# A one-token attention and feed-forward kernel: looping the query stage and the first head, loading w_down early, multiplying the last V rows directly

## The chip, the cores and the metric

The kernel runs on one core of one Trainium2 chip. The metric is device time in microseconds (us) of one execution. Engines are PE (TensorE), VectorE (DVE in the profile), ScalarE (ACT), GpSimd (POOL) and SyncE (SP), and the core has 16 DMA engines. The profile's span, from the first to the last instruction, was 1.8 to 2.1 us shorter than the time of the same run in the profiles told here.

## The reference, cut to what matters

```python
xn = _layernorm(x)                        # x: 1 x 448
q  = xn @ wq                              # 16 query heads of 256
scores = q . k_cache * 256 ** -0.5        # 8 key heads x 65536 x 256, bfloat16: 268 MB
o  = softmax(scores) . v_cache            # another 268 MB
A  = o @ wo
y  = (silu(xs @ w_gate) * (xs @ w_up)) @ w_down * sigmoid(xn @ w_r)   # one token, so xs = xn
out = x + A + xn + y
```

Almost all bytes are the two caches, each read once: 537 of the 549 MB that the DMA engines move. The arithmetic per byte is small.

## The kernel before

A key head is worked on in U = 4 units of 128 rows on each of 128 partitions. K and V pass through a ring of four 4 MB slots. SyncE issues a load when its slot has been freed (`FREE`). K is transposed on PE (`k_T`), copied out of PSUM by VectorE and ScalarE, and multiplied by the query (`k_QK`, `k_JT`). Phase A is the scores of the first head, phase B mixes a V unit of one head with a K unit of the next, phase C is V of the last head.

```python
def slot_item(kd, u, c, parts=None):      # one 4 MB load; waits until the ring slot was freed
    ...
    item(..., [("FREE", r - NSLOT)] if r >= NSLOT and k == 0 else ())

item("wq", [(w_area[:, 0:WQN], flat_src(A_wq, WQN), "wq")])
for u in range(U):                        # order of loads: wq, K of the first head ...
    for c in range(HC):
        slot_item("k", u, c)
    if u == U // 2 - 1:                   # ... with w_gate, w_up, half of w_down in the middle
        item("wg", [...], [("QT",)])
        item("wd_a", [(wd_a[:, :], wd_src(0), "wd")])
for t in range(NT):                       # then K, a pair of V slots, K
    slot_item("k", t + U, 0)
    pair_item(t)
    ...
item("wd_b", [(w_area[:, 0:WDN], wd_src(1), "we0")], [("FFN1",)])   # last loads of all:
for i in range(rep):                                                # w_down's second half, wo
    item(("wo_end", i), ...)

# The query stage: 112 matmuls, unrolled, every address fixed
for b in range(n):
    rr, c = divmod(b, 2 * half)
    ...
    ins = mm(ps_m[0:P, C_Q + lo:C_Q + lo + half + 1:half],
             lhsT=w_area[:, o:o + Dh].rearrange("p (x f) -> p x f", f=NH)[:, :, c % NH],
             rhs=xnT_sb[:, x0:x0 + 2], start=(b == 0), stop=(b == n - 1), skip_group_check=True)

def turn_A(u):                            # phase A on PE: a loop over pairs of units
    first = (u // 2) * 2 * SETS
    for c in range(HC):
        k_slots(sets_of(u, c), first)
    if u % 2:                             # the pipeline is emptied after every second unit
        n = (u + 1) * SETS
        k_JT(n - 2); k_QK(n - 1); k_JT(n - 1)

def ending():                             # (cut) after the last V rows
    dve_ob(T)                             # copy the accumulators out of PSUM
    pe_oT(T)                              # transpose, scale
    pe_ffn2(1, "wd_b", w_area)            # y, second half: 7 matmuls
    ...                                   # base row += y
    for i in range(rep):
        W_item("pe", ("wo_end", i))
        O("pe", ("FIN", i), lambda it, i=i: attn_mm(ps_fin, wo_end[:, :], [i], i == 0, i == rep - 1))
    ...                                   # RESULT = ps_fin + base row; one store from SyncE
```

## Time and profile before

| what | value |
|---|---|
| time, median of four runs | 1282.55 us (1282.35 to 1282.99) |
| DMA | 549 MB at 429 GB/s, 16 engines busy from 1.8 us to about 1272 us |
| PE / VectorE / ScalarE busy | 76% / 46% / 36% |
| first V pair issued | 101.75 us |
| last load (second part of wo) landed | 1275.7 us |
| end of the span | 1281.15 us |

The page's slices of the kernel before (40 equal slices of the span; a digit is the busy share in tenths, the last row is the DMA rate):

```profile
span 1281.2 us, 22851 instructions
DMA  9999999999999999999999999999999999999997
GB/s 406 424 436 424 450 426 427 431 431 439 436 438 417 437 430 441 432 430 428 432 446 426 436 424 436 430 444 430 428 428 433 441 436 430 425 435 431 434 437 310
```

The DMA row is full up to the last slice. The Trainium skill (DMA: Bandwidth & Descriptors, Specifications) gives a fabric ceiling of 435 GB/s; 429 over the whole span agrees with it. So time can be won only after the last bytes, and it is lost wherever the queue has nothing to do.

The timeline of PE in the kernel before, at the start (start in us, length, engine, line, operation, output and inputs, count, and in brackets the idle time before it with what ended it):

```profile
13.90 3.15 PE L367 MATMUL ps_m<-xnT_sb,w_area 128*128 128x2 bf16 x112 [1.63 <-ACT xnT_sb L355]
22.79 5.59 PE L367 MATMUL ps_t<-ident_f,ring 128*128 128x128 f32 x32 [5.74 <-DMA ring<-in_A_k_cache_dram]
...
71.06 5.35 PE L367 MATMUL ps_t<-ident_f,ring 128*128 128x128 f32 x32 [4.14 <-DMA ring<-in_A_k_cache_dram]
```

The query stage takes 3.15 us, or 28 ns per matmul. Then PE waits 5.74 us for keys, and later, before the third unit, another 4.14 us. Between those two waits PE is the slower partner: a set of 16 transposes comes every 2.53 us, a slot has four sets, so 10.1 us a slot, while a slot's 4.19 MB take 9.8 us at 429 GB/s. In phase A PE therefore never catches up by itself. The ring and the loads queued ahead hide that.

The tail of the kernel before, from the timeline (weight loads and interleaved lines left out):

```profile
1272.80 0.60 PE L367 MATMUL ps_o<-ring,p_sb 128*4 128x512 bf16 x4 [0.66 <-DMA ring<-in_A_v_cache_dram]
1273.45 0.69 DVE L555 CAST ob_sb<-ps_o 100x512 bf16<-100x512 f32 x1 [50.85 <-PE ps_o L367]
...
1274.69 2.77 PE L367 MATMUL ps_t<-w_area,hT_sb 128*1 128x448 bf16 x7 [0.22 <-DMA w_area<-in_B_w_down_dram]
...
1277.26 1.70 PE L367 MATMUL ps_s<-wo_end,oT_sb 128*1 128x448 bf16 x4
...
1278.99 0.61 DVE L742 TENSOR_TENSOR res_bf<-ps_s,rowsf 1x448 bf16<-1x448 f32 x1 [0.82 <-PE ps_s L367]
1279.63 0.32 SPq L791 DMA_DIRECT2D out_dram<-res_bf  x1
```

Eviction, w_down's matmuls, output matmuls, addition and store follow one another, 8.35 us from the release of the last V rows to the end.

### The profile page before, as it was taken

How to read it: one execution, taken by the hardware profiler on the slowest of the kernel's cores; microseconds unless marked ns; L12 is line 12 of the kernel's file. 1: busy time of each engine (PE TensorE's matmuls, PEld its weight loads, DVE VectorE, ACT ScalarE, POOL GpSimd, SP SyncE). 2: the span in 40 equal slices, each digit the busy share in tenths (PEclk: the TensorE clock that was granted, in tenths of full speed). 3: DMA queues.
4: the chain of work that ended last, by engine and by line, in shares of the span. 5: the costliest groups of instructions: out<-in, count | busy, mean ns of one | idle time of the engine just before them, and what ended most of it. 6: DMA issues, size and time to landing. Idle time of an engine off the chain costs nothing.

```text
span 1281.2 us, 22851 instructions
## 1 busy us (share of the span) xinstructions
PE 971.8 (76%) x9824; PEld 668.1 (52%) x9824; DVE 584.6 (46%) x1091; ACT 459.4 (36%) x655; POOL 4.5 (0%) x35
## 2 busy tenths in 40 slices
PE   3988777788777778677797678786778876777845
PEld 3867555455454555454664445554445644445511
DVE  4756444454444454344554344553345543445300
ACT  2645333353333443224443233432334433334300
POOL 1000000000000000000000000000000000000000
PEclk9988887898888898878888889988898888889776
DMA  9999999999999999999999999999999999999997
GB/s 406 424 436 424 450 426 427 431 431 439 436 438 417 437 430 441 432 430 428 432 446 426 436 424 436 430 444 430 428 428 433 441 436 430 425 435 431 434 437 310
DMA packets 17908, 549.22 MB, mean 429 GB/s; under 512 B 1891, under 2 KB 3942, under 8 KB 4710
## 3 DMA queue, kind: packets, MB, share of 16 engines
q1 hardware_dynamic: 17890, 549.04, 99.5%
q8 instruction: 8, 0.13, 0.0%
q14 instruction: 6, 0.05, 0.0%
q10 hardware_dynamic: 4, 0.00, 0.0%
HBM read 549.03 MB, written 0.00 MB: 429 GB/s over the span
## 4 chain that ended last, share of the span: by engine, by line
DMA 69%; PE 30%; SPq 0%; ACT 0%; issue 0%; DVE 0%
DMA ring<-in_A_k_cache_dram 64%; PE ps_t L367 23%; PE ps_q L367 5%; DMA w_area<-in_B_w_down_dram 3%; DMA ring<-in_A_v_cache_dram 2%; PE ps_s L367 1%; PE ps_m L367 1%; SPq L791 0%; ACT s L445 0%; DVE res_bf L742 0%; PE ps_o L367 0%
## 5 line engine op out<-in xcount | busy, mean ns | idle before, releaser
L367 PE MATMUL ps_t<-ident_f,ring 128*128 128x128 f32 x4096 | 551.1, 290 | 118.1 <-DMA ring<-in_A_k_cache_dram 99.1
L421 DVE COPY kt_buf<-ps_t 128x1024 bf16<-128x1024 bf16 x768 | 488.3, 683 | 272.2 <-PE ps_t L367 271.8
L367 PEld LDWEIGHTS ps_t<-ident_f,ring 128*128 128x128 f32 x4096 | 478.4, 148 | 225.4 <-DMA ring<-in_A_k_cache_dram 118.5
L423 ACT ACTIVATE kt_buf<-ps_t 128x1024 bf16<-128x1024 bf16 x256 | 262.1, 1024 | 261.6 <-PE ps_t L367 261.6
L367 PE MATMUL ps_o<-ring,p_sb 128*4 128x512 bf16 x2048 | 189.5, 533 | 148.4 <-DMA ring<-in_A_v_cache_dram 148.3
L445 ACT ACTIVATE s<-ps_q 98x512 bf16<-98x512 f32 x256 | 152.9, 597 | 274.9 <-PE ps_q L367 274.9
L367 PEld LDWEIGHTS ps_o<-ring,p_sb 128*4 128x4 bf16 x2048 | 55.3, 104 | 253.9 <-issue 228.5
L367 PE MATMUL ps_q<-kt_buf,q_cur 128*2 128x512 bf16 x2048 | 164.7, 399 | 0.0
L527 DVE RECIPROCAL rs<-ps_m 128x4 f32<-128x4 f32 x29 | 5.3, 182 | 225.5 <-PE ps_m L367 225.5
L512 ACT ACTIVATE p_sb<-S_sb 128x128 bf16<-128x128 bf16 x64 | 18.9, 307 | 244.8 <-PE ps_o L367 244.5
L367 PEld LDWEIGHTS ps_s<-sel_bf,s 128*128 128x128 bf16 x1024 | 59.9, 98 | 53.8 <-ACT s L445 50.8
L367 PE MATMUL ps_s<-sel_bf,s 128*128 128x8 bf16 x1024 | 64.0, 168 | 22.6 <-ACT s L445 22.6
L555 DVE CAST ob_sb<-ps_o 100x512 bf16<-100x512 f32 x29 | 20.1, 692 | 117.6 <-PE ps_o L367 117.6
L591 DVE TENSOR_TENSOR rowsf<-ps_m,rowsf 1x448 f32<-1x448 f32 x28 | 17.1, 611 | 53.9 <-PE ps_m L367 53.9
L367 PEld LDWEIGHTS ps_m<-rowsum,ones_f 128*128 128x128 f32 x116 | 21.6, 262 | 22.3 <-issue 22.3
L367 PEld LDWEIGHTS ps_q<-kt_buf,q_cur 128*2 128x2 bf16 x2048 | 27.1, 79 | 10.1 <-issue 5.0
L367 PE MATMUL ps_m<-wo_cur,oT_sb 128*1 128x448 bf16 x112 | 25.7, 352 | 0.0
L367 PE MATMUL ps_m<-rowsum,ones_f 128*128 128x2 f32 x116 | 24.0, 312 | 0.0
L367 PEld LDWEIGHTS ps_m<-wo_cur,oT_sb 128*1 128x1 bf16 x112 | 9.3, 83 | 13.6 <-issue 1.7
L469 DVE CAST S_sb<-ps_s 128x256 bf16<-128x256 f32 x32 | 12.9, 404 | 4.3 <-PE ps_s L367 4.3
L502 ACT ACTIVATE S_sb<-S_sb,negmax 128x512 bf16<-128x512 bf16 x16 | 13.4, 864 | 3.4 <-DVE negmax L496 3.4
L471 DVE TENSOR_REDUCE m1p<-S_sb 128x2 f32<-128x256 bf16 x32 | 13.5, 421 | 1.1
(79 smaller groups left out, 137.5 us busy)
## 6 DMA issues: line engine op xcount, KB each, us to landing
ring<-in_A_k_cache_dram SPq DMA_DIRECT2D x64, 4096.0 KB, 26.4
ring<-in_A_v_cache_dram SPq DMA_DIRECT2D x2, 4096.0 KB, 32.0
ring<-in_A_v_cache_dram SPq DMA_DIRECT2D x2, 2048.0 KB, 27.5
w_area<-in_A_wq_dram SPq DMA_DIRECT2D x1, 3584.0 KB, 11.3
wo_cur<-in_A_wo_dram SPq DMA_DIRECT2D x7, 448.0 KB, 16.0
ring<-in_A_v_cache_dram SPq DMA_DIRECT2D x2, 1024.0 KB, 29.6
ring<-in_A_v_cache_dram SPq DMA_DIRECT2D x4, 512.0 KB, 30.8
w_area<-in_B_w_gate_dram SPq DMA_DIRECT2D x1, 1568.0 KB, 38.6
```

The lines of the kernel that those rows point to most:

```text
L367: return pe.matmul(*a, **k)
L421: O(e, ("EV", s, m), lambda it: nc.vector.tensor_copy(out=kt[:, :], in_=tb[:, :]), f"ev{m}")
L423: O(e, ("EV", s, m), lambda it: nc.scalar.activation(out=kt[:, :], in_=tb[:, :], func=ACTF.Copy), f"ev{m}")
L445: O("act", ("EVQ", s), lambda it: nc.scalar.activation(out=s2[s % 2][0:QROWS, :], in_=ps_q[0:QROWS, :], func=ACTF.Copy), "evq")
L469: O("dve", ("SCOPY", u), lambda it: nc.vector.tensor_copy(out=S, in_=ps_sn))
L471: O("dve", ("SMAX", u), lambda it: nc.vector.tensor_reduce(out=m1p[:, :, k], in_=S.rearrange("p n i -> p i n"), axis=AX.X, op=ALU.max))
L502: O("act", ("EXP", h, i), lambda it, i=i: nc.scalar.activation(out=S_sb[:, :, i], in_=S_sb[:, :, i], func=ACTF.Exp, bias=negmax[:, i:i + 1 ...
L512: O("act", ("PC", t, c), lambda it: nc.scalar.activation(out=p_sb[:, c, :, :], in_=S_sb[:, n:n + CH, :], func=ACTF.Copy), "pc")
L527: O("dve", ("RS", t), lambda it: nc.vector.reciprocal(out=rs[:, :, :], in_=ps_m[0:P, C_TOT:C_TOT + NH * rep]))
L555: O("dve", ("OB", t), lambda it: nc.vector.tensor_copy(out=ob_sb[0:OROWS, :], in_=ps_o[0:OROWS, :]))
L591: O("dve", ("RES", t), lambda it: nc.vector.tensor_tensor(out=base_f, in0=ps_m[0:1, C_BIG:C_BIG + D], in1=base_f, op=ALU.add))
```

## The change

Its intent is a shorter tail (w_down's second half out of it, the last rows without the eviction, an output split over two column groups, two stores), and fewer instructions (loops on VectorE, ScalarE and in the query stage). Cut to its core:

```diff
-LAST = [32, 16, 8, 8]
+LAST = [32, 16, 8, 4, 4]
+DIRECT = 2
+NF = 2
-    LOOPS = {"pe": {"A": 2, "B": 1, "C": 2}, "dve": {"B": U}, "act": {"B": U}}
+    LOOPS = {"pe": {"A": 2, "B": 1, "C": 2}, "dve": {"A": 1, "B": (1, U)}, "act": {"A": 1, "B": U}}
 # loads: all of w_down in the first head
-            item("wd_a", [(wd_a[:, :], wd_src(0), "wd")])
+            item("wd", [(wd_a[:, :], wd_src(0), "wd"), (wo_end[:, :], wd_src(1)[:, 0:WON], "wd"),
+                        (w_area[:, WGN:WGN + WDN - WON], wd_src(1)[:, WON:WDN], "wd")])
-    item("wd_b", [(w_area[:, 0:WDN], wd_src(1), "we0")], [("FFN1",)])
 # query stage: a loop over rr, addresses from a register
+                with pe.Fori(0, n) as rr:
+                    for c in range(c0, c0 + half):
+                        w = w_area[:, bass.ds(rr * HqDh + (c // NH) * Dh, Dh)]
+                        mm(ps_m[...], lhsT=w.rearrange(...)[:, :, c % NH],
+                           rhs=xnT_sb[:, bass.ds(rr * 2 + z0, 2)], start=False, stop=False, ...)
 # phase A: every unit alike, so that VectorE and ScalarE can loop; PE empties after each
-        first = (u // 2) * 2 * SETS
         for c in range(HC):
-            k_slots(sets_of(u, c), first)
-        if u % 2:
-            n = (u + 1) * SETS
-            k_JT(n - 2) ...
+            k_slots(sets_of(u, c), u * SETS)
+        n = (u + 1) * SETS
+        k_JT(n - 2) ...
 # last two pieces of a split V slot: V as weights, straight into the output columns
+                if k > len(LAST) - 1 - DIRECT:
+                    ... mm(ps_m[0:P, C_OT + ...], lhsT=kv[:, j, :]...[:, :, hf], rhs=p_sb[:, c, o0 + j, :], ...)
 # middle, before V of the last head: both halves of y, base row put into PSUM
-        pe_ffn2(0, "wd_a", wd_a)
+        for s in range(2):
+            pe_ffn2(s)
+        ... BASE; FIN_BASE; OT_ZERO
 # ending: 8 output matmuls of 224 columns in two column groups, a copy, two stores
+        O("dve", "RESULT", lambda it: nc.vector.tensor_copy(out=res_bf[0:FROWS, :], in_=ps_s[0:FROWS, 0:DQ]))
+        for e, g in late:                 # ("sp", 0), ("act", 1)
+            prog[e].append(("d", ..., (out[0][:, g * DQ:(g + 1) * DQ], res_bf[32 * g:32 * g + 1, :]), "out"))
```

More of the change, by code (lines that the diff above doesn't have):

```diff
@@ L69, in bass_parallel_sum__gqa_block_cached__moe_arch_mod__decode_kernel @@
     WQN, WGN, WDN, WON = RP * HqDh // 2, RP * F, FH * D, rep * NH * D
-    assert WQN >= max(WGN, WDN)
+    WD4 = WON // D
+    assert WQN >= WGN + (FH - WD4) * D and FH > WD4 and D % NG == 0
     sb = []
@@ L118, in bass_parallel_sum__gqa_block_cached__moe_arch_mod__decode_kernel @@
     xn_bf = S_("xn_bf", [1, D], BF16)
-    res_bf = S_("res_bf", [1, D], BF16)
+    res_bf = S_("res_bf", [P, D // NF], BF16)
     stat = S_("stat", [1, 16], FP32)
@@ L134, in bass_parallel_sum__gqa_block_cached__moe_arch_mod__decode_kernel @@
     ps_sn = ps_s[:, 0:SBN * rep].rearrange("p (n i) -> p n i", i=rep)
-    ps_fin = ps_s[0:1, 0:D]
+    DQ = D // NF
+    FROWS = 32 * (NF - 1) + 1
     ps_o = PS_("ps_o", [P, 2 * Dh], FP32)
@@ L149, in SEM @@
         return name
-    for n_ in ["pe", "act", "dve", "pool", "qk", "jt", "evq", "exp", "pc", "qc", "w0", "out", "wq", "wg", "wo", "wd", "we0", "we1", "we2"]:
+    for n_ in ["pe", "act", "dve", "pool", "qk", "jt", "evq", "exp", "pc", "qc", "w0", "out", "wq", "wg", "wo", "wd", "we0", "we1"]:
         SEM(n_)
@@ L180, in bass_parallel_sum__gqa_block_cached__moe_arch_mod__decode_kernel @@
     items = {}
+    late = []
     semtot = {}
@@ L256, in bass_parallel_sum__gqa_block_cached__moe_arch_mod__decode_kernel @@
             slot_item("v", t, c, last_parts(rounds[0]) if rounds[0] % NSLOT == NSLOT - 1 else None)
-    item("wd_b", [(w_area[:, 0:WDN], wd_src(1), "we0")], [("FFN1",)])
     for i in range(rep):
-        item(("wo_end", i), [(wo_view(wo_end[:, :])[:, i, :, :], wo_src(Hkv - 1)[:, i, :, :], "we%d" % (i + 1))])
-    W("sp", "RESULT")
-    prog["sp"].append(("d", here[0], ("OUT",), (out[0], res_bf[:, :]), "out"))
-    items["out"] = ("out", 16)
-    W("sp", "DMA", "out")
+        item(("wo_end", i), [(wo_view(wo_end[:, :])[:, i, :, :], wo_src(Hkv - 1)[:, i, :, :], "we%d" % i)],
+             [("FFN2", 1)] if i == 0 else ())
+    for g, e in enumerate(("sp", "act")):
+        late.append((e, g))
+    items["out"] = ("out", 16 * NF)
     def W_item(e, key):
@@ L274, in pool_setup @@
         O("pool", "z_sel2", lambda it: v.memset(sel2_bf[:, :, :], 0.0))
+        O("pool", "z_m1p", lambda it: v.memset(m1p[:, :, :], 0.0))
         O("pool", "z_zero", lambda it: v.memset(zero_bf[:, :], 0.0))
@@ L298, in dve_setup @@
         v = nc.vector
+        W("dve", "z_m1p")
         O("dve", "XEZ", lambda it: v.memset(xe_row[:, :, :, :], 0.0))
@@ L382, in pe_setup @@
         W_item("pe", "wq")
+        O("pe", "QT_START", lambda it: mm(ps_m[0:P, C_Q:C_Q + NH * rep], lhsT=ident_bf[:, :], rhs=zero_bf[:, 0:NH * rep], start=True, stop=False,
+                                          skip_group_check=True), "jt", 2)
         def qt(it):
             half = Hq * NH // 2
-            n = RP * half
-            for b in range(n):
-                rr, c = divmod(b, 2 * half)
-                lo = c % half
-                x0 = 2 * rr if c < half else 2 * NE + 2 * rr
-                o = rr * HqDh + (c // NH) * Dh
-                ins = mm(ps_m[0:P, C_Q + lo:C_Q + lo + half + 1:half],
-                         lhsT=w_area[:, o:o + Dh].rearrange("p (x f) -> p x f", f=NH)[:, :, c % NH],
-                         rhs=xnT_sb[:, x0:x0 + 2], start=(b == 0), stop=(b == n - 1), skip_group_check=True)
-            return ins
-        O("pe", "QT", qt)
+            for n, c0, z0 in ((NE, 0, 0), (NE - 1, half, 2 * NE)):
+                with pe.Fori(0, n) as rr:
+                    for c in range(c0, c0 + half):
+                        lo = c % half
+                        w = w_area[:, bass.ds(rr * HqDh + (c // NH) * Dh, Dh)]
+                        mm(ps_m[0:P, C_Q + lo:C_Q + lo + half + 1:half],
+                           lhsT=w.rearrange("p (x f) -> p x f", f=NH)[:, :, c % NH],
+                           rhs=xnT_sb[:, bass.ds(rr * 2 + z0, 2)], start=False, stop=False, skip_group_check=True)
+            return mm(ps_m[0:P, C_Q:C_Q + NH * rep], lhsT=ident_bf[:, :], rhs=zero_bf[:, 0:NH * rep], start=False, stop=True, skip_group_check=True)
+        O("pe", "QT", qt, "qk", 2)
         W("pe", "PSQ_ZERO")
@@ L464, in dve_scopy @@
     def dve_scopy(u):
-        k = u % U
         W("dve", "JT", u * SETS + SETS - 1)
         W("dve", "PC", u - U, HC - 1)
-        S = S_sb[:, k * SBN:(k + 1) * SBN, :]
-        O("dve", ("SCOPY", u), lambda it: nc.vector.tensor_copy(out=S, in_=ps_sn))
+        at = lambda it, n: bass.ds(it * n, n)
+        O("dve", ("SCOPY", u), lambda it: nc.vector.tensor_copy(out=S_sb[:, at(it, SBN), :], in_=ps_sn))
         W("dve", "SCOPY", u)
-        O("dve", ("SMAX", u), lambda it: nc.vector.tensor_reduce(out=m1p[:, :, k], in_=S.rearrange("p n i -> p i n"), axis=AX.X, op=ALU.max))
-        if u >= U - 1:
-            W("dve", "SMAX", u)
-            W("dve", "M1T", u - 1)
-            O("dve", ("M1", u), lambda it: nc.vector.tensor_reduce(out=m1[:, :], in_=m1p[:, :, 0:k + 1], axis=AX.X, op=ALU.max))
+        O("dve", ("SMAX", u), lambda it: nc.vector.tensor_reduce(
+            out=m1p[:, :, at(it, 1)], in_=S_sb[:, at(it, SBN), :].rearrange("p n i -> p i n"), axis=AX.X, op=ALU.max))
+        W("dve", "SMAX", u)
+        W("dve", "M1T", u - 1)
+        O("dve", ("M1", u), lambda it: nc.vector.tensor_reduce(out=m1[:, :], in_=m1p[:, :, :], axis=AX.X, op=ALU.max))
     def pe_m1t(b):
@@ L494, in pe_bc @@
         W("dve", "BC", b)
-        W("dve", "EXP", h - 1, rep - 1)
         O("dve", ("NEGMAX", b), lambda it: nc.vector.tensor_scalar(out=negmax[:, :], in0=ps_m[0:P, C_BC:C_BC + rep], scalar1=-1.0,
@@ L535, in pe_V, with f @@
             W_item("pe", key)
-            def f(it, ap=ap, o0=o0, J=J):
+            def f(it, ap=ap, o0=o0, J=J, k=k):
                 kv = ap.rearrange("p (j d) -> p j d", d=Dh)
+                if k > len(LAST) - 1 - DIRECT:
+                    for j in range(J):
+                        for hf in range(NH):
+                            ins = mm(ps_m[0:P, C_OT + hf * rep:C_OT + (hf + 1) * rep],
+                                     lhsT=kv[:, j, :].rearrange("p (d f) -> p d f", f=NH)[:, :, hf], rhs=p_sb[:, c, o0 + j, :],
+                                     start=False, stop=False, skip_group_check=True)
+                    return ins
                 for j in range(0, J, 2):
@@ L545, in f @@
                 return ins
-            O("pe", ("PVC", t, c) if k == len(got) - 1 else ("PV", t, c, k), f)
+            O("pe", ("PV", t, c, k), f)
+        alias("pe", "PVC", t, c)
         alias("pe", "FREE", r)
@@ L552, in dve_ob @@
     def dve_ob(t):
-        W("dve", "PVC", t, HC - 1)
+        W("dve", *(("PVC", t, HC - 1) if t < NU - 1 else ("PV", t, HC - 1, len(LAST) - 1 - DIRECT)))
         W("dve", "OT", min(t, NT) - 1)
@@ L565, in f @@
                     lhsT = ob_sb[0:OROWS, n2 * Dh:(n2 + 1) * Dh].rearrange("r (p f) -> r p f", f=NH)[:, :, hf]
-                    ins = mm(ps_m[0:P, c:c + rep], lhsT=lhsT, rhs=sel2_bf[0:OROWS, n2, :], start=(n2 == 0), stop=(n2 == 1))
+                    ins = mm(ps_m[0:P, c:c + rep], lhsT=lhsT, rhs=sel2_bf[0:OROWS, n2, :],
+                             start=(n2 == 0 and t < NT), stop=(n2 == 1), skip_group_check=(t >= NT))
             return ins
@@ L641, in pe_ffn_hT, with pe_ffn2 @@
             out=hT_sb[:, :, :], in_=ps_m[0:P, C_HT:C_HT + FK].rearrange("p (t s) -> p t s", s=2)))
-    def pe_ffn2(s, key, area):
-        W_item("pe", key)
+    def pe_ffn2(s):
+        W_item("pe", "wd")
         W("pe", "HT")
@@ L648, in f @@
             for t in range(FH):
-                ins = mm(ps_y, lhsT=hT_sb[:, t, s:s + 1], rhs=area[:, t * D:(t + 1) * D],
+                area, o = (wd_a, t) if s == 0 else (wo_end, t) if t < WD4 else (w_area, WGN // D + t - WD4)
+                ins = mm(ps_y, lhsT=hT_sb[:, t, s:s + 1], rhs=area[:, o * D:(o + 1) * D],
                          start=(s == 0 and t == 0), stop=(s == 1 and t == FH - 1), skip_group_check=True)
@@ L676, in turn_A @@
     def turn_A(u):
-        first = (u // 2) * 2 * SETS
         here[0] = ("A", u)
         for c in range(HC):
-            k_slots(sets_of(u, c), first)
-        if u % 2:
-            n = (u + 1) * SETS
-            k_JT(n - 2)
-            k_QK(n - 1)
-            k_JT(n - 1)
+            k_slots(sets_of(u, c), u * SETS)
+        n = (u + 1) * SETS
+        k_JT(n - 2)
+        k_QK(n - 1)
+        k_JT(n - 1)
     def turn_B(t):
@@ L705, in turn_B, with fin @@
         k_JT(s1 - 1)
+    def fin(g):
+        return ps_s[32 * g:32 * g + 1, 0:DQ]
     def middle():
@@ L716, in middle @@
         pe_ffn_hT()
-        pe_ffn2(0, "wd_a", wd_a)
+        for s in range(2):
+            pe_ffn2(s)
+        W("dve", "FFN2", 1)
+        W("dve", "SIG")
+        W("dve", "RES", NT - 1)
+        O("dve", "BASE", lambda it: nc.vector.scalar_tensor_tensor(out=base_f, in0=ps_y, scalar=stat[0:1, 6:7],
+                                                                  in1=base_f, op0=ALU.mult, op1=ALU.add))
+        W("pe", "BASE")
+        W("pe", "SCOPY", NU - 1)
+        O("pe", "FIN_BASE", lambda it: [mm(fin(g), lhsT=ones_f[0:1, 0:1], rhs=base_f[0:1, g * DQ:(g + 1) * DQ], start=True, stop=False,
+                                           tile_position=(0, 32 * g), skip_group_check=True) for g in range(NF)][-1])
+        O("pe", "OT_ZERO", lambda it: mm(ps_m[0:P, C_OT:C_OT + NH * rep], lhsT=ident_bf[:, :], rhs=zero_bf[:, 0:NH * rep], start=True, stop=True,
+                                      skip_group_check=True))
     def turn_C(t):
@@ L728, in ending, with f @@
         pe_oT(T)
-        pe_ffn2(1, "wd_b", w_area)
-        W("dve", "FFN2", 1)
-        W("dve", "SIG")
-        W("dve", "RES", NT - 1)
-        O("dve", "BASE", lambda it: nc.vector.scalar_tensor_tensor(out=base_f, in0=ps_y, scalar=stat[0:1, 6:7],
-                                                                  in1=base_f, op0=ALU.mult, op1=ALU.add))
         W("pe", "OTSB", T)
-        W("pe", "SCOPY", NU - 1)
         for i in range(rep):
             W_item("pe", ("wo_end", i))
-            O("pe", ("FIN", i), lambda it, i=i: attn_mm(ps_fin, wo_end[:, :], [i], i == 0, i == rep - 1))
-        W("dve", "FIN", rep - 1)
-        W("dve", "BASE")
-        O("dve", "RESULT", lambda it: nc.vector.tensor_tensor(out=res_bf[:, :], in0=ps_fin, in1=base_f, op=ALU.add))
+            def f(it, i=i):
+                wo = wo_view(wo_end[:, :])
+                for hf in range(NH):
+                    for g in range(NF):
+                        ins = mm(fin(g), lhsT=oT_sb[:, hf, i:i + 1], rhs=wo[:, i, hf, g * DQ:(g + 1) * DQ], start=False,
+                                 stop=(i == rep - 1 and hf == NH - 1), tile_position=(0, 32 * g), skip_group_check=True)
+                return ins
+            O("pe", ("FIN", i), f)
+        W("dve", "FIN", rep - 1)
+        O("dve", "RESULT", lambda it: nc.vector.tensor_copy(out=res_bf[0:FROWS, :], in_=ps_s[0:FROWS, 0:DQ]))
+        for e, g in late:
+            W(e, "RESULT")
+            prog[e].append(("d", here[0], ("OUT", g), (out[0][:, g * DQ:(g + 1) * DQ], res_bf[32 * g:32 * g + 1, :]), "out"))
+        W("sp", "DMA", "out")
     pool_setup()
@@ L791, in do, with loop @@
                 eng.dma_start(fn[0], fn[1]).then_inc(sems[sem], 16)
-        def loop(body, period):
+        def loop(body, period, inner=1):
             its = {}
@@ L823, in loop @@
                 assert all(v is None or v[0] == sem for v in vals), (e, rows[1][j], vals)
-                assert all(nums[i] == nums[0] + i * step for i in range(n)), (e, rows[1][j], nums)
+                per = 1
+                if inner > 1 and any(nums[i] != nums[0] + i * step for i in range(n)):
+                    per, step = inner, nums[inner] - nums[0]
+                assert all(nums[i] == nums[0] + i // per * step for i in range(n)), (e, rows[1][j], nums)
                 assert nums[0] >= 1 and step >= 0, (e, rows[1][j], nums)
@@ L832, in loop @@
                     continue
-                if period > 1 and step % period == 0 and nums[0] - sub[j] * (step // period) >= 1:
+                if per > 1:
+                    rk = (nums[0], step, None)
+                elif period > 1 and step % period == 0 and nums[0] - sub[j] * (step // period) >= 1:
                     rk = (nums[0] - sub[j] * (step // period), step // period, True)
@@ L844, in loop, with turn @@
             waited.clear()
-            with eng.Fori(0, n) as it:
+            def turn(it):
                 for j, (kind, lab, key, fn, sem) in enumerate(rows[0]):
@@ L854, in loop @@
                         for rk, r in regs.items():
-                            if rk[2] or j + 1 == len(sub):
+                            if rk[2] or rk[2] is False and j + 1 == len(sub):
                                 eng.reg_add(r, r, rk[1])
+            with eng.Fori(0, n // inner) as it:
+                if inner == 1:
+                    turn(it)
+                else:
+                    with eng.Fori(0, inner) as k:
+                        turn(k)
+                    for rk, r in regs.items():
+                        if rk[2] is None:
+                            eng.reg_add(r, r, rk[1])
             waited.clear()
@@ L866, in emit @@
                     k2 += 1
-                loop(entries[k:k2], period)
+                loop(entries[k:k2], *(period if isinstance(period, tuple) else (period,)))
                 k = k2
```

## The prediction

> **What bounds the kernel.** The DMA stream. The page's slices show the 16 DMA engines at 9 tenths or more in 39 of 40 slices, 549 MB at a mean of 429 GB/s, while PE is 76% busy and VectorE 46%. The Trainium skill (DMA: Bandwidth & Descriptors, Specifications) gives a fabric ceiling of 435 GB/s; 429 over a span that includes start and end agrees, so the body has nothing to give. Packet records show no stretch below 80% between the first microseconds and the tail. What the change can move is the start, the tail, and places where a late buffer release would let the queue run dry.
>
> **The tail before** (timeline): the last V piece releases PE at 1272.80, w_down's second half at 1274.69, wo_end lands at about 1275.7. Then in series: 7 w_down matmuls (2.77 us at half clock), 4 output matmuls until 1278.96, the result addition 0.61 us, the store issued at 1279.63, end 1281.2. So 5.5 us lie between the last data and the end.
>
> **What the change does.**
> 1. The second w_down half (784 KB, about 1.9 us of stream) moves from the end of the queue to the first head. Bytes are unchanged, so the stream ends when it did; but the last V piece then lands only about 1.1 us ahead of wo_end (PE released near 1274.7), and the 2.77 us of w_down matmuls leave the tail.
> 2. The last 8 rows are two pieces of 4, multiplied with V as weights straight into the output columns, so the ps_o eviction (0.69 us) goes off the chain. Estimate for 8 direct and 4 transposing matmuls: 0.9 us (112 similar query matmuls took 3.15 us at full clock; the tail runs at half).
> 3. Output matmuls: 8 of 224 columns in two column groups, estimated 0.95 us against 1.70, since the scores' 8 of 512 columns in four groups took 0.62 us. The base row is already in PSUM; the result copy is 33x224, estimated 0.37 us against 0.61.
> 4. Two stores of 448 bytes on two queues: no gain in themselves; the last 1.5 us from issue to end stays.
>
> Sum: V 1274.7, OTSB ready 1275.8, FIN 1275.9 to 1276.9, copy to 1277.3, end 1278.8: about 2.4 us saved. Against it: 2 KB and smaller packets cost about 0.2 us of stream (4 KB packets ran at 405 GB/s, 32 KB ones at 431).
>
> 5. Loops on VectorE and ScalarE, and in the query stage: both have slack, so no direct gain. Fewer instructions are fetched: the page shows 14 instruction packets, and 16 KB ones took about 1.05 us of one DMA engine. The Trainium skill (Runtime: NRT & Kernel Launch, Instruction fetch mechanics) describes this autonomous 16 KiB refill; the trace's packet size agrees. Worth 0 to 1 us, as the slowest engine sets the end.
> 6. PE now drains after every unit of the first head (about 3 us twice), and the middle stage gains about 3 us before V of the last head starts. The second delays the issue of a V pair (1227.79 before) which the fastest engines need only 1 to 3 us later. I expect at most 0.5 us lost, on the fast engines, which are not last.
>
> **Prediction:** 1280.2 us, 8 in 10 between 1278.7 and 1281.7. Faster by over 2%: 0.01; within 2%: 0.985; slower: 0.005.
>
> **Right if:** the stream's rate and end stay (429 GB/s, last weights landing near 1275.5); the tail's chain reads V, direct matmuls, OTSB, FIN, copy, store with no w_down; FIN takes about 1 us; instruction packets fall. **Wrong if:** packets show a gap near 1231 or 100 to 110 us; the 448-byte stores or ScalarE's issue take over 2 us; the column groups do not overlap (FIN 1.7 us); or an instruction fetch stalls PE or ScalarE in the unrolled tail.

## The result, and the profile after

The changed kernel took 1286.24 us (median of four runs, 1284.79 to 1286.62) against 1282.55 us. The ratio of 1.0026, with a 95% interval of 1.0009 to 1.0044, is the mean time of one kernel's runs over that of the other's of the same rounds, so it is not quite the ratio of these medians. The prediction was 1280.2 us and its range ended at 1281.7. The profile is of the fastest run, 1284.79 us.

The page's slices of the kernel after:

```profile
span 1283.0 us, 23236 instructions
DMA  9998999999999999999999999999999999999998
GB/s 407 428 427 378 428 421 435 429 446 423 441 420 435 428 442 429 441 422 433 444 427 429 430 431 433 444 427 431 428 432 437 441 427 425 433 433 443 423 436 351
```

The fourth slice, 96 to 128 us, fell from 424 to 378 GB/s. The table of stretches shows it closely, first before, then after. Columns: the stretch in us, its length, busy time and count of PE, PE weight loads, VectorE, ScalarE, GpSimd, then PE's granted clock, DMA share and GB/s. A packet is counted where it starts, so a share may exceed 1.

```profile
109.00:111.00 2.00, 2.00 (x26) 1.51 (x25) 1.35 (x4) 1.06 (x3) 0.00 (x0) 1.00 1.21 524
111.00:113.00 2.00, 1.43 (x20) 0.87 (x18) 1.84 (x3) 1.06 (x2) 0.00 (x0) 1.00 0.98 426
```

```profile
109.00:111.00 2.00, 2.00 (x24) 1.92 (x20) 1.44 (x4) 1.59 (x2) 0.00 (x0) 1.00 0.23 98
111.00:113.00 2.00, 2.00 (x26) 1.52 (x24) 1.35 (x3) 1.26 (x2) 0.00 (x0) 1.00 0.00 0
```

All DMA engines stood still, from 111.3 to 114.6 us, while PE worked. From the packet records, with each packet cut at the borders of the stretch, I worked out 4.64 us of idle time per engine on average between 90 and 130 us; before it was 0. This number is called the gap from here on. The last data landed 4.4 us later (packets ended at 1279.7 us against 1275.3).

Why was the queue empty? The next load, the first V pair, was issued late. SyncE's issues, before and then after:

```profile
101.75 0.33 SPq L791 DMA_DIRECT2D ring<-in_A_v_cache_dram  x1
```

```profile
113.67 0.33 SPq L826 DMA_DIRECT2D ring<-in_A_v_cache_dram  x1
```

That issue waits for PE to have transposed two K slots, so it shows how late PE is. The waits of SyncE's queue name it, before and then after (line, what it waited for, then us in total, times, longest):

```profile
SPq L785 <- PE ps_t L367: 19.9, 1, 19.9
```

```profile
SPq L820 <- PE ps_t L374: 23.3, 1, 23.3
```

PE's timeline after, at the start:

```profile
14.06 2.09 PE L374 MATMUL ps_m<-xnT_sb,w_area 128*128 x16 [0.23 <-issue]
16.64 2.10 PE L374 MATMUL ps_m<-xnT_sb,w_area 128*128 x16 [0.49 <-issue]
...
29.29 2.10 PE L374 MATMUL ps_m<-xnT_sb,w_area 128*128 x16 [0.44 <-issue]
31.46 0.18 PE L374 MATMUL ps_m<-zero_bf,ident_bf 128*128 128x4 bf16 x1
```

The looped query stage takes 17.3 us (14.06 to 31.39) instead of 3.15. Its matmuls start 131 ns apart (2.10 us for 16). The keys had landed long before, and the first transposes begin at 32.84 us instead of 22.79.

The tail after:

```profile
1279.09 0.38 PE L374 MATMUL ps_m<-p_sb,ring 128*128 128x2 bf16 x8 [0.25 <-DMA ring<-in_A_v_cache_dram]
...
1279.77 0.16 DVE L592 TENSOR_TENSOR oT_sb<-ps_m,rs 128x4 bf16<-128x4 f32 x1 [0.59 <-PE ps_m L374]
...
1279.99 0.91 PE L374 MATMUL ps_s<-wo_end,oT_sb 128*1 128x224 bf16 x8 [0.25 <-DVE oT_sb L592]
1280.94 0.38 DVE L773 CAST res_bf<-ps_s 33x224 bf16<-33x224 f32 x1 [1.01 <-PE ps_s L374]
1281.35 0.32 SPq L826 DMA_DIRECT2D out_dram<-res_bf  x1
1281.36 0.23 ACTq L826 DMA_DIRECT2D out_dram<-res_bf  x1
```

It is as designed. From the last packet's end to the end of the span it takes 3.3 us (1279.7 to 1283.0) instead of 5.8 (1275.3 to 1281.15): 2.5 us won. The last data came 4.4 us later: 4.4 - 2.5 = 1.9 us, the growth of the span.

### The profile page after: what moved, and what is told of

Same layout as the page of the kernel before. It is cut to its first block, busy times and chain, and to the rows that moved or that the text cites. A ratio compares the mean times of both kernels' runs of the same rounds, so it can differ in the third digit from the quotient of the medians.

```text
span 1283.0 us, 23236 instructions
## 1 busy us (share of the span) xinstructions
PE 1000.2 (78%) x9859; PEld 680.5 (53%) x9859; DVE 585.5 (46%) x1094; ACT 459.3 (36%) x655; POOL 4.6 (0%) x36
## 4 chain that ended last, share of the span: by engine, by line
DMA 64%; PE 33%; issue 1%; ACT 1%; DVE 1%; SPq 0%; DVEq 0%; ACTq 0%
DMA ring<-in_A_k_cache_dram 59%; PE ps_t L374 25%; PE ps_q L374 6%; DMA ring<-in_A_v_cache_dram 5%; PE ps_m L374 2%; PE ps_s L374 1%; ACT s L454 1%; DMA wr_row<-in_B_w_r_dram 0%; SPq L826 0%; DVE kt_buf L430 0%; DVE rowsf L342 0%; DVE xe_row L337 0%; DVE stat L314 0%; DVE rowsf L321 0%; ACTq L826 0%
## 5 line engine op out<-in xcount | busy, mean ns | idle before, releaser
L374 PE MATMUL ps_t<-ident_f,ring 128*128 128x128 f32 x4096 | 563.1, 292 | 104.8 <-DMA ring<-in_A_k_cache_dram 83.5
L477 DVE CAST S_sb<-ps_s 128x256 f32 x32 | 12.9, 404 | 9.0 <-PE ps_s L374 9.0
L374 PE MATMUL ps_m<-xnT_sb,w_area 128*128 x112 | 14.7, 184 | 2.9 <-issue 2.9
L479 DVE TENSOR_REDUCE m1p<-S_sb x32 | 13.5, 422 | 4.4
```

What stands on the lines that cost most here:

```text
L374: return pe.matmul(*a, **k)
L477: O("dve", ("SCOPY", u), lambda it: nc.vector.tensor_copy(out=S_sb[:, at(it, SBN), :], in_=ps_sn))
L479: O("dve", ("SMAX", u), lambda it: nc.vector.tensor_reduce(out=m1p[:, :, at(it, 1)], in_=S_sb[:, at(it, SBN), :].rearrange("p n i -> p i n ...
```

## The experiments

**Theory.** The loss is one gap near 110 us. PE is late there for two reasons that add up: the looped query stage (10 us late at the first transposes) and the emptying of PE's pipeline after every unit. **Rivals.** Either one alone is enough; or VectorE's and ScalarE's loops, or the early w_down, are to blame; or the whole stream became slower.

The intervals of the ratios are about 0.3% wide, or 4 us. Those of a_pipe2, b_qt_loop, b_wd_early, a_flat_nodirect and a_flat_onequeue include 1, so their times alone do not tell them from the kernel before; there the traces carry the reading.

### a_qt_flat: the change, with the query stage unrolled

```diff
-                with pe.Fori(0, n) as rr:
+                for rr in range(n):
                     ...   # and fixed addresses instead of bass.ds(rr * ...)
```

> The changed kernel with its query stage unrolled again (112 matmuls with fixed addresses); everything else of the change stays, the drain of PE after each unit of the first head too. Theory: the looped query stage took 18 us instead of 3, so the first transposes began at 32.8 us instead of 22.8, and with the two extra drains the first V pair was issued at 113.7 us, after the DMA queue had run dry near 110 us. Expect here: query stage 3 us, first transpose near 23 us, V pair issued near 106 us, no gap in the DMA packets, time 1280.0 us (1279 to 1281). Rival 1 (the per-unit drain and the loops on VectorE and ScalarE alone make PE late): gap stays, time above 1283. Rival 2 (the stream itself became slower through smaller packets or early w_down): no change from 1285 to 1286.

Measured: 1280.31 us (1279.68 to 1280.80) against 1282.96, ratio 0.9978 (0.9962 to 0.9995). The gap is gone, and the V pair is issued at 107.48 us, 1.5 us later than I expected:

```profile
13.61 3.13 PE L374 MATMUL ps_m<-xnT_sb,w_area 128*128 128x2 bf16 x112
...
107.48 0.33 SPq L826 DMA_DIRECT2D ring<-in_A_v_cache_dram  x1
```

The stream did not become slower, and VectorE's and ScalarE's loops with PE's emptying don't make the gap alone. The rest of the change wins what was predicted for it.

### a_pipe2: the change, with the units of the first head paired again

```diff
-    "dve": {"A": 1, "B": (1, U)}, "act": {"A": 1, "B": U}
+    "dve": {"B": (1, U)}, "act": {"B": U}
     # turn_A as in the kernel before; the looped query stage stays
```

> As a_pipe, mended: the score columns of the first head are addressed by the unit and not by the turn. The changed kernel with the first head's units paired on PE (drain after every second unit only) and VectorE and ScalarE unrolled there; the looped query stage stays. Theory (query loop 10 us and drains about 3 us each add up, and only the sum passes the slack): V pair issued near 107.5 to 109 us against 113.7; gap 0 to 1 us of mean engine time instead of 4.6; time 1279.5 to 1281.5. Rival (the query loop alone is enough): gap 3 us or more, time above 1283.

Measured: 1281.26 us (1280.62 to 1281.62) against 1282.84, ratio 0.9986 (0.9971 to 1.0002). The gap is 0.23 us, with the V pair at:

```profile
108.17 0.33 SPq L828 DMA_DIRECT2D ring<-in_A_v_cache_dram  x1
```

So the looped query stage alone does not make a gap of this size either. The kernel is still about 1 us slower than a_qt_flat; its last packet ended at 1276.5 us instead of 1275.4. In its profile (of the slowest of its four runs) the trace points to one late DMA engine and not to a slower stream: of the 16 completion marks of the last load, 15 came by 1275.90 us and the last at 1276.94, their mean is 1275.44 against 1275.37 in a_qt_flat, and from 1275.5 us on the last packets end one at a time, 0.07 us apart. Why that engine was late is not shown. About three engines stood still in the small gap, but the packet records don't name engines, so whether it was one of those can't be seen.

### a_flat_pipe2: both undone

> The fourth corner of the two by two: the changed kernel with both costs of the first head undone (query stage unrolled; units paired, VectorE and ScalarE unrolled there). Theory: with the query stage unrolled there was no gap left near 110 us to close, so the time is that of a_qt_flat, 1280.3 us, within 0.6; the V pair is issued near 104 us instead of 107.5. Rival (the drain costs time even without a gap): 1279.5 or less.

Measured: 1280.11 us (1279.68 to 1280.25) against 1283.01, ratio 0.9977 (0.9961 to 0.9994). V pair at 105.17 us, no gap. As expected, emptying the pipeline costs nothing visible while there is no gap. This is the fastest median of a correct kernel, level with a_qt_flat.

### b_qt_loop: the kernel before, with the looped query stage alone

> The kernel before with the looped query stage alone. Theory: query stage 18 us, first transpose near 33 us, the 4 us that PE waited for the third unit's keys absorb a part, V pair issued near 107.7 us where the queue runs dry from about 107.5 us (w_down's second half is not ahead of it here): gap 0 to 1.5 us, time 1282.5 to 1284. Rival (the query loop alone makes the whole loss): a gap of 4 us and more, time above 1286.

Measured: 1283.82 us (1283.11 to 1284.30) against 1282.96, ratio 1.0005 (0.9989 to 1.0022). The gap is 1.25 us, the queue beginning to run dry at 107.6 us, with the V pair at:

```profile
108.59 0.33 SPq L793 DMA_DIRECT2D ring<-in_A_v_cache_dram  x1
```

The query stage takes 17.3 us here too, but most of it is hidden.

### b_qt_drain: the kernel before, with the looped query stage and the emptying after each unit

```diff
 # on top of b_qt_loop
-            k_slots(sets_of(u, c), first)
-        if u % 2:
-            ...
+            k_slots(sets_of(u, c), u * SETS)
+        n = (u + 1) * SETS
+        ...   # emptied after every unit
```

> The kernel before with both of the suspected costs and none of the rest: the looped query stage, and PE's drain after every unit of the first head. Theory (the two add up, and the stream ahead of the first V pair sets the slack): the V pair is issued near 113 us as in the changed kernel, but without w_down's second half (1.9 us of stream) ahead of it the queue runs dry 1.9 us earlier: a gap of 6 to 7 us of mean engine time, time 1288.5 to 1290. Rival (the gap belongs to something else of the change, VectorE's or ScalarE's loops or the early w_down): gap as in the looped query stage alone, 1.3 us, time below 1285.

Measured: 1288.80 us (1287.57 to 1289.90) against 1282.88, ratio 1.0049 (1.0033 to 1.0066). The profiled run took 1288.16 us with a gap of 5.09 us; time and mechanism came as expected, the gap in that profile was 1 us smaller than I expected. (What makes the gap vary is shown at a_same1 and a_same2 below; near the emptyings of this profile PE ran at half clock once, from 102.9 to 106.3 us.) Its V pair and its stretches:

```profile
112.43 0.33 SPq L791 DMA_DIRECT2D ring<-in_A_v_cache_dram  x1
```

```profile
109.00:111.00 2.00, 2.00 (x26) 1.52 (x25) 1.86 (x3) 1.06 (x2) 0.00 (x0) 1.00 0.00 0
111.00:113.00 2.00, 2.00 (x26) 1.51 (x25) 1.50 (x3) 1.09 (x2) 0.00 (x0) 1.00 0.00 0
```

Nothing of the tail, the early w_down or the loops on VectorE and ScalarE is in this kernel, and the whole loss is. The two costs together are the cause. The early w_down even helps here: its 1.9 us of stream lie ahead of the V pair, so the queue begins to run dry at 109.5 us with it and at 107.6 without.

The profiled runs side by side (starts of the first transposes of a unit, from the timeline):

| kernel | units 1 to 4 start, us | V pair issued | gap, us | median time |
|---|---|---|---|---|
| before | 22.8, 44.1, 71.1, 92.1 | 101.75 | 0 | 1282.6 |
| a_flat_pipe2 | 22.8, 44.7, 73.2, 95.5 | 105.17 | 0 | 1280.1 |
| a_qt_flat | 22.6, 46.1, 73.2, 97.0 | 107.48 | 0 | 1280.3 |
| a_pipe2 | 33.0, 54.1, 77.5, 98.5 | 108.17 | 0.23 | 1281.3 |
| b_qt_loop | 33.3, 54.5, 77.9, 98.9 | 108.59 | 1.25 | 1283.8 |
| b_qt_drain | 33.2, 57.5, 80.0, 102.0 | 112.43 | 5.09 | 1288.8 |
| after | 32.8, 57.7, 81.0, 103.2 | 113.67 | 4.64 | 1286.2 |

A late start of 10 us shrinks to 6 or 7 us at the third unit, against the kernel before, where the units are paired, because PE had waited 4.14 us there before. Emptying after the first unit takes that cushion away (a_qt_flat reaches the third unit no later than a_flat_pipe2, since both wait there for keys; after does not wait). Emptying after the third unit then adds to the rest.

### a_same1, a_same2: the changed kernel again

> The changed kernel again, for its profile: its profiled run took 1284.8 us, the other three 1286.0 to 1286.6. If the length of the gap near 110 us makes the difference, a run of 1286 us shows the gap at 5.5 to 6.5 us of mean engine time instead of 4.6; if not, the gap is 4.6 again and the time is lost elsewhere (second gap near 1231 us, or a slower end of the slowest DMA engine).

> The changed kernel once more, for the same question as a_same1: gap 5.5 to 6.5 us in a run of 1286 us, 4.6 in one of 1284.8.

Measured, single runs: 1286.15 us with a gap of 5.81 us (V pair at 114.89), and 1286.31 us with a gap of 6.16 us (V pair at 115.20). In these three profiles the longer the gap, the longer the time. Where PE lost the extra 1.2 to 1.5 us is in the clock column. The stretches after the first, second and third emptying, in the run of 1284.79 us and then in a_same2:

```profile
57.00:61.00 4.00, 3.31 (x29) 2.77 (x29) 2.39 (x6) 2.17 (x3) 0.00 (x0) 1.00 0.98 404
81.00:85.00 4.00, 4.00 (x36) 3.48 (x40) 3.27 (x8) 2.05 (x2) 0.00 (x0) 1.00 0.97 418
104.00:108.00 4.00, 4.00 (x26) 4.00 (x25) 2.82 (x6) 1.70 (x2) 0.00 (x0) 0.63 0.97 418
```

```profile
57.00:61.00 4.00, 3.98 (x21) 3.98 (x22) 2.86 (x6) 1.02 (x1) 0.00 (x0) 0.57 0.99 408
81.00:85.00 4.00, 3.82 (x20) 3.85 (x21) 2.42 (x6) 1.02 (x1) 0.00 (x0) 0.57 0.95 410
104.00:108.00 4.00, 3.49 (x21) 3.42 (x22) 2.34 (x5) 1.48 (x2) 0.00 (x0) 0.63 0.95 410
```

In the slower run PE restarts at half clock after each emptying, in the faster one only after the third. The Trainium skill (TensorE: Matmul & The Clock Gate, Part 1) describes something close to this: the clock is halved after an idle window of about 3.4 us, and the windows run freely, so the same kernel meets them at a different phase in each run. The trace agrees on the windows: the halved stretches in its clock record are 3.41 us long, and in a_same2 they begin at 57.27, 81.16 and 105.05 us, in the run of 1284.79 us only at 103.58. It does not agree on "idle". The transposes of two units stand 3.4 to 3.9 us apart, but PE works on in between. Before the first halving of a_same2:

```profile
53.79 0.63 PE L374 MATMUL ps_q<-kt_buf,q_cur 128*2 128x512 bf16 x8
55.12 0.26 PE L374 MATMUL ps_s<-sel_bf,s 128*128 128x8 bf16 x4 [0.71 <-ACT s L454]
55.34 0.63 PE L374 MATMUL ps_q<-kt_buf,q_cur 128*2 128x512 bf16 x8
56.68 0.26 PE L374 MATMUL ps_s<-sel_bf,s 128*128 128x8 bf16 x4 [0.71 <-ACT s L454]
```

In the 3.41 us before each of its three halvings PE was busy 1.9, 1.5 and 2.0 us, started at most three transposes, and paused for 0.71 us at most. How little work is little enough is not shown.

### a_qt_static: what makes the looped stage slow (wrong result)

```diff
-                        w = w_area[:, bass.ds(rr * HqDh + (c // NH) * Dh, Dh)]
+                        w = w_area[:, (c // NH) * Dh:(c // NH) * Dh + Dh]
-                           rhs=xnT_sb[:, bass.ds(rr * 2 + z0, 2)], ...
+                           rhs=xnT_sb[:, z0:z0 + 2], ...
```

> Wrong result on purpose: the query stage keeps its loops, but every matmul in them has a fixed address, so no register is computed between matmuls. Tells apart what makes a looped matmul take 131 ns from start to start instead of 28: if the register instruction ahead of each one (46 ns in the trace), the 16 matmuls of an iteration take about 0.5 us and the stage about 6.5 us (0.45 us remain between iterations), the V pair is issued near 107.5 and the time is below 1281.5; if the loop itself, the stage stays at 18 us and the time at 1285 to 1286.5.

Measured, one run: 1279.80 us, and the whole stage, loops included, in 3.23 us:

```profile
14.01 3.23 PE L374 MATMUL ps_m<-xnT_sb,w_area 128*128 128x2 bf16 x112
```

So looping is nearly free, 0.08 us over the unrolled stage before, and the 0.45 us between iterations that I had put down to the loop vanished too. The cost is the address from a register. The instructions at the line of the matmul helper in the changed kernel show what stands between the matmuls (operation and count, then shortest, median and longest time in ns, then first and last start in us):

```profile
L374 PE MATMUL ps_m<-xnT_sb,w_area x112: 164/185/187, 14.1 to 31.2; 128*128 x112
L374 PEldq FUSED_REGOPS  x108: 46/46/51, 14.1 to 31.1; - x108
```

A register operation of 46 ns goes ahead of nearly every matmul, and the spacing is 131 ns instead of 28. The other 57 ns per matmul, and the 0.45 us at the start of an iteration, come with it; the trace does not name them.

### a_flat_late: closing a second, smaller gap

With the query stage unrolled, the queue still ran short near 1231 us: 0.76 us of mean idle time between 1215 and 1255 us, because both halves of y and the base row now stand before V of the last head. This kernel moves the second half and the base row into PE's wait before the last V pair.

```diff
-        for s in range(2):
-            pe_ffn2(s)
-        ... BASE, FIN_BASE, OT_ZERO
+        pe_ffn2(0)
...
     for t in range(NT, NU):
         turn_C(t)
+        if t == NT + 1:
+            ... pe_ffn2(1), BASE, FIN_BASE, OT_ZERO
```

> A candidate to beat both: query stage unrolled, and the second half of the w_down product with the base row moved from before the last head's V to the 20 us in which PE waits for the last V pair (PE's loop over the last head is unrolled for it). With the query stage alone unrolled the DMA queue ran dry for 0.76 us of mean engine time near 1231 to 1234 us, because the V pair of the third unit was issued at 1233.1. Theory: issued near 1229 here, no gap there, time 0.5 to 0.9 us below 1280.3: 1279.3 to 1279.9. Rival (that gap falls on engines that are not last and costs nothing): 1280.2 to 1280.5.

Measured: 1280.75 us (1280.46 to 1281.05) against 1282.84, ratio 0.9984 (0.9971 to 0.9998). The gap closed (no idle time there, V pair at 1229.55 instead of 1233.08 us), and the time did not fall: my expectation missed, the rival held. The reason shows in the 16 completion marks of the first wo load. In a_flat_late, without the gap, they came from 1272.28 to 1275.45 us, spread over 3.2 us (in the kernel before from 1272.26 to 1275.17); in a_qt_flat, with the gap, from 1274.52 to 1275.26. The gap held back the early engines and left the last one where it was, so here it cost nothing. That a gap shorter than the spread of the engines is always free is not shown: in b_qt_loop the gap of 1.25 us never stopped all engines (at least one was always at work, and 3 or more nearly all of the time), and the last packet still ended at 1276.9 us instead of the 1275.3 of the kernel before. The gap at 110 us of the changed kernel stopped every engine.

### b_wd_early, a_flat_nodirect, a_flat_onequeue: what the tail's parts are worth

b_wd_early is the kernel before with w_down's second half loaded and multiplied early, and nothing else changed in the tail:

> The kernel before with one part of the change alone: the second half of w_down is loaded in the first head and multiplied before the last head's V; the tail is otherwise as before. Theory: w_down's 2.8 us leave the tail, but V's last piece lands 1.9 us later, and the eviction, the output matmuls (1.7 us), the addition (0.6 us) still follow it: 0.5 us saved if the stream ends where it did, less up to 0.5 us for the later V pair near 1231: time 1282.0 to 1283.0. Rival (the early w_down is the main gain of the tail): 1280.5 or less.

Measured: 1282.27 us (1281.67 to 1282.36) against 1282.84, ratio 0.9995 (0.9979 to 1.0010). As expected it is worth about half a microsecond, which the interval does not resolve: 2.8 us of matmuls leave the tail, but the last V rows are released at 1274.70 instead of 1272.80 us, because bytes were moved, not saved.

a_flat_nodirect is a_qt_flat without the direct rows:

```diff
-LAST = [32, 16, 8, 4, 4]
-DIRECT = 2
+LAST = [32, 16, 8, 8]
+DIRECT = 0
```

> The changed kernel with the query stage unrolled (1280.3 us) and without the direct last rows (pieces of 32, 16, 8, 8 rows, all through the accumulators). Theory: from the last piece's release to the scaled output 1.9 us (as in b_wd_early) instead of 0.85, so the time is 0.8 to 1.2 us above the same kernel with direct rows: 1281.0 to 1281.5, and 0.8 to 1.0 us below b_wd_early (1282.3). Rival (the landing of the last weights sets the end): 1280.3 to 1280.6.

Measured: 1281.70 us (1281.16 to 1282.17) against 1282.88, ratio 0.9993 (0.9977 to 1.0010), 1.4 us above a_qt_flat, which ran on another chip, and 0.2 us above the range that I expected. The traces give a steadier number: from the release of the last piece to the end of the scaled output it takes 1.86 us (1274.27 to 1276.13) here and 0.84 us in a_qt_flat (1274.77 to 1275.61). So in the traces direct rows are worth 1.0 us.

a_flat_onequeue is a_qt_flat with both stores issued by SyncE:

> The changed kernel with the query stage unrolled and both halves of the result stored from SyncE's queue, one after the other, instead of one from SyncE and one from ScalarE. Theory: the second store is issued about 0.4 us after the first (issues stand 0.37 to 0.48 us apart in the traces), so the end comes 0.3 to 0.5 us later: 1280.6 to 1280.8, against 1280.3. Rival (the two-queue store is a main gain): 1281.3 or more.

Measured: 1280.75 us (1280.32 to 1281.34) against 1283.01, ratio 0.9984 (0.9968 to 1.0001). In the trace the second store is issued 0.37 us after the first, and from the first issue to the end it takes 1.84 us instead of 1.64: two queues are worth 0.2 us. The Trainium skill (DMA: Bandwidth & Descriptors, Issuing engines are not separate DMA queues) says that a second issuing engine saves only issue time; the trace agrees.

## Why the prediction was wrong, point by point

- **What bounds the kernel: right.** The DMA stream does, and the loss of the changed kernel is idle time of the DMA engines.
- **The tail (points 1 to 4): right.** Predicted 2.4 us saved, measured 2.5. Direct and transposing matmuls took 0.64 us from the last release (1279.09 to 1279.73), predicted 0.9; the output matmuls 0.91 (predicted 0.95); the copy 0.38 (predicted 0.37).
- **Point 5 is the step that failed: "Loops on VectorE and ScalarE, and in the query stage: both have slack, so no direct gain."** The loops on VectorE and ScalarE do no visible harm. The query stage was given no cost at all, and it went from 3.15 to 17.3 us. The prediction does not ask what PE does next: the first transposes came 10 us later, and the slack that was left ahead of the first V pair could not take that and the emptying together. Of the second half of the point, instruction packets fell only from 14 to 12; no run shows what that is worth.
- **Point 6 had about the right size, 3 us per emptying, and the wrong total.** On top of the looped query stage, the two emptyings moved the V pair by 3.8 us (b_qt_drain against b_qt_loop) to 7.0 us (a_same2 against a_pipe2, which differ in VectorE's and ScalarE's loops too), so by 1.9 to 3.5 us each. Alone, the emptying costs nothing that the runs resolve (a_qt_flat). The slack ahead of the first V pair held it and nearly held the query loop (a_pipe2), but not both. The prediction never added up what PE could be late before that issue. It did name a gap at 100 to 110 us among what would prove it wrong; it began near 109.5 us, and the next load's first packet started at 114.6.
- **The second gap** of point 6 was judged rightly: a_flat_late shows that it costs nothing.
- **The sum:** 4.4 us later data less 2.5 us of shorter tail makes +1.9 us of span in the profiled run. In typical runs the gap is 5.8 to 6.2 us instead of 4.6 and the kernel is slower by 3.7 us. With the query stage unrolled, the same change gives 1280.31 us, against the 1280.2 predicted.

The spacing of a matmul with an address from a register was open before: no trace of the kernel before showed one in a batch of small matmuls. What remains open is why one DMA engine ended about 1 us after the others in a_pipe2.

## What to carry to other kernels

Where the DMA queue is the limit, list for each load what it waits for and how long the queue ahead of it lasts, and add up every delay that the change puts on that engine before the issue. Two delays that each fit into the slack may not fit together. Before looping a stage of small matmuls, ask whether its addresses come from a register: loops with fixed addresses were free here, and register addresses made the stage more than five times as long (17.3 us against 3.15). And the end is set by the last of the 16 engines: a pause that falls on the early ones can be free (a_flat_late), but its mean over the engines does not tell you so (b_qt_loop).

## What the Trainium skill lacked or had wrong

- TensorE: Matmul & The Clock Gate (Part 1) gives a floor of about 25 ns from start to start for small matmuls, and the fixed-address query stage agrees (28 ns). In the pages that I read, none says what an address from a register costs: here 131 ns from start to start, with a register operation of 46 ns ahead of nearly each matmul.
- Runtime: NRT & Kernel Launch (Instruction fetch mechanics) calls runtime control flow expensive, for branches that leave the fetched window. The small loops here show no such cost, which does not contradict the page: the looped stage with fixed addresses took 3.23 us, the unrolled one 3.15. Its 16 KiB refill agrees with the packets here (16 KB, about 1.05 us each of one DMA engine).
- DMA: Bandwidth & Descriptors: The page says that engines 7 and 15 are usually slower than the others, but I found no figure there for how far the 16 engines of one long stream drift apart. Here the completion marks of one load spread over 2.9 us in the kernel before, and in a_qt_flat a mean pause of 0.76 us that fell on the early engines did not lengthen the run.
- The clock gate's free-running window of about 3.4 us, as the TensorE page (Part 1) has it, fits the difference between the three profiles of the changed kernel (1284.8, 1286.2 and 1286.3 us): in the first the clock was halved once near the emptyings, in the others three times. But the page gives an idle window as the condition, and in a_same2 the clock was halved after windows in which PE was busy for 1.5 to 2.0 of 3.41 us and never paused for more than 0.71 us.
